# Three-layer kernel on one core: first product cut 384 + 192 tokens, its result stored in units of 192 tokens, some weight loads and front-end steps moved

## The chip, the cores and the metric

One Trainium2 chip, one of its cores. The metric is device time in microseconds of one execution; of several executions the median is taken. The program is built with an instruction scheduler, so the order of the instructions on an engine is partly the scheduler's; the places where the kernel itself fixes an order are named below.

## The reference, cut to what matters

```python
a = phi - np.max(phi, axis=2, keepdims=True)        # phi: 8 batches, 8 heads, 576 tokens, 32 slots
a = np.exp(a)
a = a / (np.sum(a, axis=2, keepdims=True) + 1e-09)
k_m = np.einsum('bhsm,bhsd->bhmd', a, k)            # d = 64
v_m = np.einsum('bhsm,bhsd->bhmd', a, v)
scores = (1.0 / np.sqrt(64)) * np.matmul(q, k_m.transpose(0, 1, 3, 2))
scores = scores - np.max(scores, axis=-1, keepdims=True)
attn = np.exp(scores)
attn = attn / (np.sum(attn, axis=-1, keepdims=True) + 1e-09)
x = np.matmul(attn, v_m)                            # 4608 tokens x 512
...
h = x @ w_in                                        # first layer: 512 -> 2048
r = np.maximum(h, 0.0)
x = (r * r) @ w_out                                 # 2048 -> 512
...
h = x @ w_in2                                       # second layer, the same sizes
return ((h * (1.0 / (1.0 + np.exp(-h)))) @ w_out2).astype(np.float32)
```

## The kernel before, in words

The kernel has four stages: the **first product** (`x @ w_in` with its relu, together with the attention that feeds it), then the **second product** (`g @ w_out`, with g the squared relu), then the two products of the second layer. The last three use seven block products in the place of eight (their blocks are called B11, B21, B12, B22 and the combinations T1 to T4); each matmul in them has 384 columns. A full-precision product is made of three matmuls of type fp32r, on a high and a low part of each factor (hi x hi, hi x lo, lo x hi).

**First product.** Batch by batch (8 batches of 576 tokens), 16 units a batch; a unit is 128 of the 2048 columns of w_in. `first_product(t)` makes unit t: two halves of 288 tokens (`HALF`), each of 6 matmuls 128x288, so 12 matmuls a unit, into a two-bank PSUM tile `h` (two such tiles). ScalarE then applies the relu (L671) into `gt`, which holds two units (f and f + 1), and after every second unit SyncE stores `gt` to the scratch tensor g1 (`to_rows`, L623). The rows of g1 are tiles of 384 tokens, so a batch of 576 falls into a store of 384 and one of 192 tokens. Batch 0 is made otherwise (`first_by_halves`, L637): tokens 0 to 255 and 256 to 575 apart (`SPANS0`), 96 matmuls of 256 columns and 96 of 320.

**Front.** While batch b - 1 is multiplied, `front(b)` prepares batch b: loads of phi, kv and q, `kv_product` (`pskv`, L407), `kv_turn`, then for three ranges r of 192 tokens `scores(r)` (`pssc`; max, exp on ScalarE L483, sum, reciprocal, a scaling on GpSimd) and `transpose_attn(r)` (`et`, then hi by ScalarE L499 and lo by VectorE L500 into `at`, the operand of batch b's units), and four pieces `wp` of w_in multiplied by v_m (`piece`, `pswp`; hi by ScalarE L554, lo by VectorE L555). The tables `PLAN`, `PLAN1` and `PLAN2` say ahead of which unit each step is written. For batch 0, `START` and a list `tail` give the order, with small bf16 matmuls (`hot`) between as fillers. `follow(a, b)` puts a behind b in the order of their engine without a wait; `after` and `hold` add a wait (`hold` for the latest matmul begun).

**Second product.** Its steps are (block product, pair of weight rows) in the order n = 0, 1, 3, 2, 5, 4, 6, four steps for each n. A step is 12 matmuls of 384 columns (L889). Each weight tile `ws` has six slots; slots 2, 5 and 4 hold the weights for T2, B22 and T3. `begin_out1` loads them, and the first quarters `r` of g1, during the last units of the first product; loads of one queue are issued by SyncE in their order.

```python
for r in range(NR):
    at(begin + plan["q"][r], lambda r=r: load_q(r))
    at(begin + plan["scores"][r], lambda r=r: scores(r))
    at(begin + plan["attn"][r], lambda r=r: transpose_attn(r))
```

Of the kernel before, what the change touches and what calls it, by code (L numbers as in the profile page):

```python
# [26 lines left out]
HALF = S // 2  # L27
# [7 lines left out]
TB, TH = 6, 384  # L35
NQ = NF // 2
# [8 lines left out]
CHUNKS0 = ((0, P), (2 * P, 3 * P, S - P))  # L45
SPANS0 = ((0, 2 * P), (2 * P, S))


IDLE = {2: 7, 3: 6, 4: 7}
START = ("phi", "kv", "idle15", "max", "rows", "idle3", "exp", "idle18", "product", "q", "q", "w0", "w1", "q", *(f"w{n}" for n in range(2, 8)))  # L50
UNITS0 = (6, 6, 7, 7, 9, 9, 10, 10)
PIECES0 = {0: (1, 0), 1: (1, 1), 7: (2, 0), 8: (2, 1), 10: (3, 0), 12: (3, 1)}
# [3 lines left out]
    "q": (-5, -3, 5), "scores": (4, 8, 12), "attn": (6, 10, 14), "pieces": (4, 8, 12, 16),  # L56
}
PLAN1 = {
    "phi": -9, "ones": 4, "kv": (-8, -8, -8, -8), "softmax": (1, 2, 3), "product": 5, "turn": 7,
    "q": (-6.5, 4, 9), "scores": (8, 10, 11), "attn": (10, 11, 13), "pieces": (9, 12, 13, 15),  # L60
}
PLAN2 = {**PLAN, "phi": -10, "ones": -5.5, "kv": (-12, -11, -10, -9), "softmax": (-5, -4, -3)}
# [15 lines left out]
def attention_moe_moe(ctx: ExitStack, tc, q, kv, phi, w_in1, w_out1, w_in2, w_out2, out):  # L78
# [199 lines left out]
    def unit(j, i):  # L278
        ins = to_f32(win[:, j, 2 * i:2 * i + 2].rearrange("p k c -> p (k c)"), staged[j, i])
        made[j] = to_f32.last  # L280
        if begun:
            hold(ins)
        else:
            after(ins, ready[(i, 1, 2, 4)[j]])
# [25 lines left out]
    def front(b):  # L310
# [7 lines left out]
        def load_phi():  # L318
            t = st["a"] = lpool.tile([P, NC, 2 * P], F32, tag="a", bufs=2, name="a")
            n = P * (NC - 1) * 2 * P  # L320
            held = hold if b > 1 else in_order
            held(nc.sync.dma_start(t[:, :NC - 1], phi[b, :n].rearrange("(p c e) -> p c e", p=P, e=2 * P)))
            held(nc.sync.dma_start(t[:rows(NC - 1), NC - 1], phi[b, n:].rearrange("(p e) -> p e", e=2 * P)))

        def load_kv(c):


            d = 2 * D + 1
            if c == 0:
                st["kv"] = lpool.tile([P, NC, NP, 2, d], F32, tag="kv", bufs=1, name="kv")  # L330
            n = rows(c)
            t = st["kv"][:n, c]
            (hold if b > 1 else in_order)(nc.sync.dma_start(t.rearrange("p k e d -> p (k e d)"), kv[b, c * P:c * P + n]))
# [11 lines left out]
        def load_q(r):  # L345
            if b == 0:
                if r == 0:
                    st["q"] = apool.tile([P, NP, S], F32, tag="at", name="q")
                in_order(nc.sync.dma_start(st["q"][:, :, r * RT:(r + 1) * RT], q[b, r]))
                return  # L350
            t = st["q", r] = fpool.tile([P, NP, RT], F32, tag="q", bufs=2, name="q")
            (hold if begun else in_order)(nc.sync.dma_start(t, q[b, r]))
# [45 lines left out]
        def kv_product(*gs):  # L398

            ps = bank("pskv")  # L400
            for g in gs:
                st["ps", g] = (ps if g or b else bank("pskv"))[:, g, :2 * D + 1]
            for c, g in ((c, g) for c in range(NC) for g in gs):
                n = rows(c)
                for p in range(NP):
                    h = 2 * p + g
                    mm = pe(nc.tensor.matmul(  # L407
                        st["ps", g][p * M:(p + 1) * M], st["a"][:n, c, h * M:(h + 1) * M], st["kv"][:n, c, p, g],
                        start=(c == 0), stop=(c == NC - 1),
                    ))  # L410
                    join(mm, c == g == p == 0, new=True)
                if b == 0 and g and c in IDLE:
                    idle(IDLE[c])

# [36 lines left out]
        def join(mm, first, new=False):  # L451

            if first and b > 1:
                follow(mm, group["h"] if new else group["last"])
            group["last"] = mm
# [14 lines left out]
        def scores(r):  # L470

            ps = bank("pssc")[:, :, :RT]
            by_heads(ps, 0, lambda p: st["q", r][:, p], st["turned"], new=True)
            nb = 2 * RT // M
            mx = fpool.tile([P, nb, 1], F32, tag="smx", bufs=1, name="smx")
            sm = fpool.tile([P, nb, 1], F32, tag="ssm", name="ssm")
            e = fpool.tile([P, 2, RT], F32, tag="e", bufs=3, name="e")
            for g in range(2):
                nc.vector.transpose(e[:, g], ps[:, g])
            ev = e.rearrange("p g (k m) -> p (g k) m", m=M)  # L480
            nc.vector.reduce_max(mx[:, :, 0], ev, axis=AX.X)
            nc.vector.tensor_tensor(ev, ev, mx.to_broadcast([P, nb, M]), op=ALU.subtract)
            nc.scalar.activation(e, e, AF.Exp, scale=1.0 / float(D) ** 0.5)  # L483
            nc.vector.reduce_sum(sm[:, :, 0], ev, axis=AX.X)
            nc.vector.tensor_scalar_add(sm, sm, 1e-9)
            nc.vector.reciprocal(sm, sm)
            scaled.append(nc.gpsimd.tensor_tensor(ev, ev, sm.to_broadcast([P, nb, M]), op=ALU.mult))
            if r == NR - 1 and "ones" in group:
                follow(scaled[-1], group.pop("ones"))
            st["e", r] = e  # L490

        def transpose_attn(r):
# [6 lines left out]
            nc.scalar.copy(hi, x)  # L499
            nc.vector.tensor_tensor(lo, x, hi.bitcast(F32), op=ALU.subtract)  # L500

        def scores_by_token(r):

            cs = CHUNKS0[r]
            n = len(cs)
            ps = bank("pssc").rearrange("p a n -> p (a n)")[:, :n * 2 * P]
            for i, c in enumerate(cs):
                for p in range(NP):
                    to = i * 2 * P + p * 2 * M
                    pe(nc.tensor.matmul(  # L510
                        ps[:, to:to + 2 * M], st["q"][:, p, c:c + P], st["km"][:, p].rearrange("p g m -> p (g m)"),
# [9 lines left out]
            nc.vector.reduce_max(mx[:, :, :, 0], pv, axis=AX.X)  # L521
# [5 lines left out]
            nc.vector.tensor_tensor(ev, ev, sm.to_broadcast([P, 2 * nb, M]), op=ALU.mult)  # L527
            st["e", r] = e.rearrange("p (g t) -> p g t", g=2)

        def turn_attn(r):  # L530
# [5 lines left out]
            for i, c in enumerate(CHUNKS0[r]):  # L536
                for g in range(2):
                    mm = nc.tensor.transpose(ps[:, g, c - first:c - first + P], st["e", r][:, g, i * P:(i + 1) * P], ident)
                    if r == 0:
                        pe(mm)  # L540
            x = ps[:, :, :end - first]
# [4 lines left out]
        def piece(j, h=None):  # L546
# [10 lines left out]
            by_heads(ps[:, :, :PC], 1, lambda p: win[:, 2 * j + h, p], made[2 * j + h])  # L557
# [4 lines left out]
        if b == 0:  # L562
            third = iter(range(NR))
            do = {
                "phi": load_phi, "kv": lambda: [load_kv(c) for c in range(NC - 1)], "max": max_phi, "rows": max_rows,
                "exp": exp_phi, "product": lambda: kv_product(0, 1), "q": lambda: load_q(next(third)),
# [8 lines left out]
            for w in range(8, 2 * NPC):  # L575
# [3 lines left out]
                lambda: scores_by_token(0), lambda: scores_by_token(1), lambda: (unit(0, 0), unit(0, 1)),  # L579
                lambda: idle(6), lambda: piece(0, 0), lambda: idle(9), lambda: turn_attn(0), lambda: idle(5),  # L580
                lambda: (unit(1, 0), unit(1, 1)), lambda: piece(0, 1),
                lambda: turn_attn(1), lambda: (unit(2, 0), unit(2, 1)), lambda: (unit(3, 0), unit(3, 1)),
            )
            for n, fn in enumerate(tail):
                at(n - 50, fn)
            for n, t in enumerate(UNITS0):
# [29 lines left out]
    def to_rows(b, f, gt):  # L616

        fh, u = divmod(f - 1, NQ)
        i = 0
        while i < S:  # L620
            to, k = divmod(b * S + i, TH)
            n = min(TH - k, S - i)
            nc.sync.dma_start(g1[to // 2][:, 2 * fh + to % 2, u:u + 2, k:k + n], gt[:, :, i:i + n])  # L623
            i += n

    def first_by_halves(t):
# [16 lines left out]
        if half == 0:  # L643
            gts[pair] = gpool.tile([P, 2, S], F32, tag="gt", name="gt")
        nc.scalar.activation(gts[pair][:, :, tk], h[:, :, :n], AF.Relu)
# [3 lines left out]
    def first_product(t):  # L649
# [5 lines left out]
        h = psum.tile([P, 2, 512], F32, tag="h", bufs=2, name="h")  # L655
        j, fo = divmod(f * P, W4)
        for half in range(2):
            tk = slice(half * HALF, (half + 1) * HALF)
            ops = [(g, s, x) for g in range(2) for s, x in ((0, 0), (0, 1), (1, 0))]
            for k, (g, s, x) in enumerate(ops):  # L660
                mm = nc.tensor.matmul(  # L661
                    h[:, half, :HALF], wp[b, j][:, g, s, fo:fo + P], attnT[b][:, x, g, tk],
                    start=(k == 0), stop=(k == len(ops) - 1),
                )
                if half == k == 0:
                    begun.append(mm)
                group["h"] = mm
        if f % 2 == 0:
            gts[b] = gpool.tile([P, 2, S], F32, tag="gt", name="gt")
        gt = gts[b]  # L670
        relus.append(nc.scalar.activation(gt[:, f % 2].rearrange("p (h t) -> p h t", h=2), h[:, :, :HALF], AF.Relu))  # L671
# [121 lines left out]
    def second(src, order, square, to, weights, begin, tiles=tuple(range(10))):  # L793
# [76 lines left out]
        begin(quarters)  # L870
# [4 lines left out]
        for k, (b, n, h) in enumerate(steps):  # L875
            ahead(k + AHEAD)
            bank = BANKS[n]
# [7 lines left out]
            x = cc.pop((b, n, h))  # L885
            for u in range(QS):
# [29 lines left out]
    def begin_out1(quarters):  # L916
# [4 lines left out]
        def held(ins):  # L921
            nonlocal n
            hold(ins, step=min(last, last - EARLY + n * 3 // 4))
            n += 1

        for q in range(WR, WR + 2):
            for k in range(SLOTS):
# [8 lines left out]
        for k in (2, 5, 4):  # L936
            for q in range(WR + 2, NQ):
                held(load_w(w1o, q, k))
# [156 lines left out]
```

## Time and profile before

| | |
|---|---|
| median of 3 executions | 1381.91 us (1380.5 to 1383.04) |
| the profiled execution | 1379.26 us, its span 1377.4 us |
| busy share of TensorE (PE), weight loads (PEld) | 99%, 95% |
| busy share of VectorE (DVE), ScalarE (ACT) | 71%, 58% |
| granted TensorE clock | 1.00 in all stages |

The profile is of one execution; 1.9 us of its time lie outside the span. PE rows are matmuls, PEld rows the loads of their stationary operand, which overlap the matmuls. A matmul's own duration (299 ns for one of 288 columns) is longer than the distance to the next one, since matmuls are pipelined: rates are read from the length of a run of many matmuls. A matmul of type f32 stands in the trace as two instructions, one of type fp32r as one.

### The profile page before, as it was taken

The page shows a single profiled execution, that of the slowest core. Times are in us where ns is not written, and L with a number is a line of the kernel's source. Part 1 is how long each engine was busy: PE and PEld are TensorE (multiplying, and loading weights), DVE is VectorE, ACT ScalarE, POOL GpSimd, SP SyncE. Part 2 cuts the span into 40 slices and gives each one's busy share as a digit, 9 for nine tenths or more (in the row PEclk, how much of TensorE's full clock was granted, in tenths as well). Part 3 has the DMA queues.
Part 4 walks back from the last instruction along what each step waited for, and adds up shares of the span by engine and source line. Part 5 has one row for each costly group of instructions (what it writes and reads, how often), then busy time and mean ns, then how long its engine had stood idle before and what let it go on. Part 6 is the DMA issues. An engine that isn't in the chain of part 4 may idle for free.

```text
span 1377.4 us, 25465 instructions
## 1 busy us (share of the span) xinstructions
PE 1356.8 (99%) x9349; PEld 1311.7 (95%) x9349; DVE 982.6 (71%) x1602; ACT 796.1 (58%) x1305; POOL 21.5 (2%) x44
## 2 busy tenths in 40 slices
PE   8899999999999999999999999999999999999998
PEld 6778888898999999999999999999999999999998
DVE  4768787747797988989565756566449868768583
ACT  3656666667778686777354645555444444444442
POOL 0000000000000000000000000000000000000000
PEclk9999999999999999999999999999999999999999
DMA  9979999899877978899998787888999567574651
GB/s 325 373 248 339 360 362 328 294 346 356 307 256 274 310 256 299 262 310 340 301 322 299 250 308 269 281 287 285 366 399 355 165 217 244 171 238 159 223 157 35
DMA packets 208446, 388.26 MB, mean 282 GB/s; under 512 B 19264, under 2 KB 90944, under 8 KB 208320
## 3 DMA queue, kind: packets, MB, share of 16 engines
q1 hardware_dynamic: 208320, 386.62, 81.2%
q8 instruction: 74, 1.21, 0.4%
q14 instruction: 52, 0.43, 0.1%
HBM read 253.38 MB, written 133.17 MB: 281 GB/s over the span
## 4 chain that ended last, share of the span: by engine, by line
PE 88%; DMA 9%; SPq 1%; ACT 1%; DVE 1%; issue 0%; ACTq 0%; DVEq 0%
PE psa L889 22%; PE psb L889 15%; PE psa L1003 15%; PE psc L889 15%; PE h L661 9%; PE psc L1003 7%; PE psb L1003 4%; DMA st<-moe_w_in 2%; DMA a<-phi 2%; DMA g<-gt 1%; DMA w1o<-pp 1%; PE pswp L463 1%; PE pskv L407 1%; DMA q<-q 1%; DMA r<-g 1%; DMA kv<-kv 1%
## 5 line engine op out<-in xcount | busy, mean ns | idle before, releaser
L856 DVE TENSOR_TENSOR c<-r,c 128x768 fp32r<-128x768 f32 x336 | 316.5, 955 | 141.4 <-ACT c L855 140.5
L855 ACT CAST c<-r 128x768 fp32r<-128x768 f32 x336 | 279.7, 837 | 233.9 <-PE psa L889 86.1
L889 PE MATMUL psa<-c,ws 128*128 128x384 f32 x1728 | 310.7, 336 | 1.8 <-ACT c L855 1.5
L889 PEld LDWEIGHTS psa<-c,ws 128*128 128x128 f32 x1728 | 301.8, 188 | 2.4 <-ACT c L855 1.7
L1003 PE MATMUL psa<-xc,ws 128*128 128x384 f32 x1152 | 217.9, 336 | 0.0
L889 PE MATMUL psc<-c,ws 128*128 128x384 f32 x1152 | 207.9, 335 | 0.0
L661 PEld LDWEIGHTS h<-at,wp 128*128 128x128 f32 x1344 | 180.1, 188 | 28.7 <-ACT gt L671 16.7
L889 PE MATMUL psb<-c,ws 128*128 128x384 f32 x1152 | 206.3, 336 | 0.0
L1003 PEld LDWEIGHTS psa<-xc,ws 128*128 128x128 f32 x1152 | 202.3, 188 | 0.0
L889 PEld LDWEIGHTS psc<-c,ws 128*128 128x128 f32 x1152 | 201.3, 188 | 0.0
L889 PEld LDWEIGHTS psb<-c,ws 128*128 128x128 f32 x1152 | 201.2, 188 | 0.0
L661 PE MATMUL h<-at,wp 128*128 128x288 f32 x1344 | 190.9, 299 | 4.4 <-ACT gt L671 4.2
L1003 PE MATMUL psc<-xc,ws 128*128 128x384 f32 x576 | 110.8, 335 | 0.0
L1003 PEld LDWEIGHTS psc<-xc,ws 128*128 128x128 f32 x576 | 101.1, 188 | 0.0
L671 ACT ACTIVATE gt<-h 128x576 f32<-128x576 f32 x112 | 72.2, 648 | 35.7 <-PE h L661 25.9
L205 DVE TENSOR_TENSOR pp<-pw,pp 128x256 f32<-128x256 f32 x148 | 63.1, 436 | 32.7 <-ACT pp L204 30.4
L833 ACT ACTIVATE r<-r 128x768 f32<-128x768 f32 x96 | 80.7, 843 | 4.2 <-PE psc L889 3.4
L162 ACT CAST top<-st 128x256 f16<-128x256 bf16 (+1 forms) x112 | 57.9, 526 | 30.5 <-PE psa L1003 12.9
L204 ACT CAST pp<-pw 128x256 fp32r<-128x256 f32 x148 | 58.0, 402 | 29.5 <-PE psa L1003 15.4
L1017 ACT ACTIVATE g2t<-g2t 128x1152 f32<-128x1152 f32 x48 | 54.7, 1164 | 28.1 <-DVE g2t L733 28.1
L166 DVE SCALAR_TENSOR_TENSOR pw<-st,top 128x256 int32<-128x256 int32 x96 | 41.2, 435 | 28.6 <-ACT top L162 28.0
L1003 PE MATMUL psb<-xc,ws 128*128 128x384 f32 x288 | 56.9, 336 | 0.0
(103 smaller groups left out, 1164.3 us busy)
## 6 DMA issues: line engine op xcount, KB each, us to landing
r<-g SPq DMA_DIRECT2D x192, 384.0 KB, 5.8
g<-g2t SPq DMA_DIRECT2D x48, 768.0 KB, 7.0
ws<-w2i SPq DMA_DIRECT2D x136, 256.0 KB, 5.1
ws<-w2o SPq DMA_DIRECT2D x136, 256.0 KB, 4.4
ws<-w1o SPq DMA_DIRECT2D x116, 256.0 KB, 4.5
g<-gt SPq DMA_DIRECT2D x64, 384.0 KB, 5.9
kv<-kv SPq DMA_DIRECT2D x32, 516.0 KB, 6.2
st<-moe_w_out SPq DMA_DIRECT2D x64, 256.0 KB, 5.5
```

The lines of the kernel that those rows point to most:

```text
L162: ins = nc.scalar.copy(top.bitcast(F16).rearrange("p (n h) -> p n h", h=2)[:, :, 1], flat.bitcast(BF16).rearrange("p (n h) -> p n h", h=4) ...
L166: to_f32.last = nc.vector.scalar_tensor_tensor(f.bitcast(I32), flat.rearrange("p (n w) -> p n w", w=2)[:, :n, 1], 13, top, op0=ALU.logical ...
L204: held(nc.scalar.copy(hi, w[:, of]))
L205: tt(lo, w[:, of], hi.bitcast(F32), op=ALU.subtract)
L661: mm = nc.tensor.matmul(h[:, half, :HALF], wp[b, j][:, g, s, fo:fo + P], attnT[b][:, x, g, tk], start=(k == 0), stop=(k == len(ops) - 1),)
L671: relus.append(nc.scalar.activation(gt[:, f % 2].rearrange("p (h t) -> p h t", h=2), h[:, :, :HALF], AF.Relu))
L833: ins = nc.scalar.activation(x, x, AF.Square)
L855: nc.scalar.copy(c[:, 0], r(name))
L856: tt(c[:, 1], r(name), c[:, 0].bitcast(F32), op=ALU.subtract)
L889: mm = nc.tensor.matmul(ps[o][bank], W[h * QS + u][:, slot(n), wi, o * P:(o + 1) * P], x[:, xi, u], start=(first and h == u == m == 0), st ...
L1003: mm = nc.tensor.matmul(ps[q][bank], W[q][:, slot(n), wi, k * P:(k + 1) * P], x[:, xi, k], start=(n in FIRST and k == 0 and m == 0), stop= ...
L1017: nc.scalar.activation(gq[q][:, :3], gq[q][:, :3], AF.Silu)
```

## The change

- **g by units of 192 tokens.** `gt` is laid out as 3 ranges of 192 tokens, in each range both units of a pair next to each other; a store then writes runs of 2 x 192 (or 4 x 192) values where it wrote runs of 192 or 384. The second product reads its operand as two runs of 192 columns. The PSUM tile `h` is now one stretch of 576 columns that crosses the border of two banks (`HB`), and so a unit is 6 matmuls of 384 columns and 6 of 192, where it was 12 of 288.
- **Batch 0.** `SPANS0` becomes tokens 0 to 191 and 192 to 575, so 96 matmuls of 192 columns and 96 of 384. Its q is loaded in two contiguous pieces; the first units begin ahead of the second piece of w_in, and the second range's max comes behind the first range's scaling.
- **Softmax and transposes.** The exp of `scores(r)` is a step of its own (`softmax(r)`), written one unit later from batch 2 on and put behind the latest relu on ScalarE, as is the cast in `transpose_attn`; the transposes come one unit later (7, 11, 15 for 6, 10, 14). `PLAN1` and `PLAN2` change, `join` gets new cases.
- **Queues.** q is laid out contiguously for each range; loads of kv for batch 2 and phi for batch 3 are put behind the last q of batch 1.
- **Second product.** Slots 2, 5 and 4 of weight rows 4 to 7 are loaded after steps 1, 3, 5, 7, 9 and 11 of the second product; the others start up to 6 matmul groups later.

```diff
-HALF = S // 2
+HB = 512 - TH
...
-CHUNKS0 = ((0, P), (2 * P, 3 * P, S - P))
-SPANS0 = ((0, 2 * P), (2 * P, S))
+CHUNKS0 = ((0, RT - P), (RT, RT + P, S - P))
+SPANS0 = ((0, RT), (RT, S))
...
-    "q": (-5, -3, 5), "scores": (4, 8, 12), "attn": (6, 10, 14), "pieces": (4, 8, 12, 16),
+    "q": (-5, -3, 5), "scores": (4, 8, 12), "attn": (7, 11, 15), "pieces": (4, 8, 12, 16),
...
+            if b == 2:
+                follow(ins, group["q"])
...
-            nc.scalar.activation(e, e, AF.Exp, scale=1.0 / float(D) ** 0.5)
+            st["e", r] = e, ev, sm, nb
+
+        def softmax(r):
+
+            e, ev, sm, nb = st["e", r]
+            ins = nc.scalar.activation(e, e, AF.Exp, scale=1.0 / float(D) ** 0.5)
+            if b > 1:
+                follow(ins, relus[-1])
...
-            nc.scalar.copy(hi, x)
+            ins = nc.scalar.copy(hi, x)
+            if b > 1:
+                follow(ins, relus[-1])
...
+            at(begin + plan["scores"][r] + (1 if b > 1 else 0), lambda r=r: softmax(r))
...
-            to, k = divmod(b * S + i, TH)
-            n = min(TH - k, S - i)
-            nc.sync.dma_start(g1[to // 2][:, 2 * fh + to % 2, u:u + 2, k:k + n], gt[:, :, i:i + n])
-            i += n
+            to, half = divmod(b * NR + j, 2)
+            n = min(2 - half, NR - j)
+            rows = g1[to // 2][:, 2 * fh + to % 2, u:u + 2].rearrange("p u n -> p (u n)")
+            nc.sync.dma_start(
+                rows[:, half * 2 * RT:(half + n) * 2 * RT], gt[:, j:j + n].rearrange("p j u n -> p (j u n)"),
+            )
+            j += n
...
-        h = psum.tile([P, 2, 512], F32, tag="h", bufs=2, name="h")
+        h = psum.tile([P, 2, 512], F32, tag="h", bufs=2, name="h").rearrange("p a n -> p (a n)")[:, HB:HB + S]
         j, fo = divmod(f * P, W4)
-        for half in range(2):
-            tk = slice(half * HALF, (half + 1) * HALF)
+        for tk in (slice(0, TH), slice(TH, S)):
...
-        relus.append(nc.scalar.activation(gt[:, f % 2].rearrange("p (h t) -> p h t", h=2), h[:, :, :HALF], AF.Relu))
+        relus.append(nc.scalar.activation(gt[:, :, f % 2], h.rearrange("p (j n) -> p j n", n=RT), AF.Relu))
...
-                            ps[o][bank], W[h * QS + u][:, slot(n), wi, o * P:(o + 1) * P], x[:, xi, u],
+                            ps[o][bank].rearrange("p (j n) -> p j n", n=RT) if square else ps[o][bank],
+                            W[h * QS + u][:, slot(n), wi, o * P:(o + 1) * P], x[:, xi, u],
...
-        for k in (2, 5, 4):
-            for q in range(WR + 2, NQ):
-                held(load_w(w1o, q, k))
+        return {
+            4 * i + 2 * j + 1: [lambda k=k, q=q: hold(load_w(w1o, q, k)) for q in (WR + 2 * j, WR + 2 * j + 1)]
+            for i, k in enumerate((2, 5, 4)) for j in range(2)
+        }
```

Three places show what moves. The first is TensorE in the middle of batch 0, where batch 1's kv product (`pskv`), its turn (`pst`), pieces of w_in (`pswp`) and batch 0's units (`h`) alternate. Before:

```order
L637 MATMUL h<-at,wp 128x320 x12
L407 MATMUL pskv<-kv,a 32x129 x40
L463 MATMUL pswp<-win,kvm 32x256 x8
L637 MATMUL h<-at,wp 128x256 x2
L637 MATMUL h<-at,wp 128x320 x2
L435 MATMUL pst<-ident,y_604 128x128 x2
```

And now:

```order
L677 MATMUL h<-at,wp 128x192 x12
L481 MATMUL pswp<-win,kvm 32x256 x8
L677 MATMUL h<-at,wp 128x384 x12
L423 MATMUL pskv<-kv,a 32x129 x40
L677 MATMUL h<-at,wp 128x192 x12
L677 MATMUL h<-at,wp 128x384 x12
L451 MATMUL pst<-ident,y_643 128x128 x2
```

The piece stands 12 matmuls ahead of the kv product, and 24 whole matmuls of units stand between the kv product and its turn, where there were 4.

The second place is SyncE's queue late in batch 0: the stores of g, the last q of batch 1 and the five loads of kv for batch 2. Before:

```order
L333 DMA kv<-kv 128x1032 x4
L333 DMA kv<-kv 64x1032
L623 DMA g_0_100<-gt 128x2x384
L352 DMA q<-q 128x768
L623 DMA g_0_100<-gt 128x2x192
```

And now:

```order
L661 DMA g_0_100<-gt 128x768
L661 DMA g_0_100<-gt 128x384
L365 DMA q<-q 128x768
L338 DMA kv<-kv 128x1032 x4
L338 DMA kv<-kv 64x1032
```

The q load has moved ahead of the five kv loads.

The third place is ScalarE at the last range of attention, that of batch 7 (`e` the exp, `at` the cast of the transposed attention, `gt` the relu of one unit). Before:

```order
L554 CAST wp<-pswp 128x2x512
L483 ACTIVATE e<-e 128x384
L162 CAST top<-st 128x256
L671 ACTIVATE gt<-h 128x576
L162 CAST top<-st 128x256
L671 ACTIVATE gt<-h 128x576
L204 CAST pp<-pw 128x256
L499 CAST at<-et 128x2x192
L671 ACTIVATE gt<-h 128x576 x2
```

And now:

```order
L713 ACTIVATE gt<-h 128x3x192
L506 ACTIVATE e<-e 128x384
L162 CAST top<-st 128x256
L713 ACTIVATE gt<-h 128x3x192
L204 CAST pp<-pw 128x256
L713 ACTIVATE gt<-h 128x3x192
L524 CAST at<-et 128x2x192
L713 ACTIVATE gt<-h 128x3x192
L587 CAST wp<-pswp 128x2x512
```

Counted from the end of the first product, 18 relus stood behind this `at` cast before and 17 stand behind it now; batch 7 itself has 16.

## Rows read from the trace of the kernel before

**Rows 1.** Windows: length, busy us (instructions) of PE, PEld, DVE, ACT, POOL, clock, DMA.

```profile
20.00:35.80 15.80, 12.24 (x127) 9.09 (x126) 12.49 (x23) 9.13 (x15) 0.00 (x0) 1.00 1.04 373
35.80:74.60 38.80, 35.36 (x434) 27.96 (x434) 29.53 (x65) 25.04 (x42) 2.58 (x5) 1.00 0.97 355
74.60:158.00 83.40, 79.98 (x926) 67.74 (x919) 58.04 (x135) 52.59 (x103) 5.66 (x9) 1.00 0.90 317
158.00:290.00 132.00, 132.00 (x1460) 114.99 (x1459) 105.24 (x240) 90.44 (x175) 10.36 (x15) 1.00 0.95 331
290.00:320.00 30.00, 27.18 (x199) 26.15 (x198) 4.72 (x10) 20.69 (x33) 0.00 (x0) 1.00 1.02 365
```

**Rows 2.** Waits of PE, 35.8 to 320 us: us in total, times, longest.

```profile
PE h L661 <- ACT gt L671: 4.2, 6, 1.1
PE pssc L463 <- DMA q<-q: 1.5, 1, 1.5
PE psa L889 <- ACT c L855: 1.5, 1, 1.5
PE h L637 <- ACT wp L559: 1.2, 1, 1.2
PE pswp L463 <- DVE e L479: 0.5, 1, 0.5
PE psa L889 <- DVE c L856: 0.4, 1, 0.4
```

**Rows 3.** The chain, one row; then PE's timeline in four short windows: start, length, run.

```profile
453.69 8.36 PE psc L889 x48
...
36.64 2.65 PE L637 MATMUL h<-at,wp 128*128 128x320 f32 x17
215.82 4.41 PE L661 MATMUL h<-at,wp 128*128 128x288 f32 x32
30.95 2.31 PE L637 MATMUL h<-at,wp 128*128 128x256 f32 x18
18.16 2.29 PE L510 MATMUL pssc<-km,q 128*128 128x64 f32 x19
```

**Rows 4.** Groups by shape, PE and PEld, first 325 us: busy, mean ns, idle before.

```profile
L661 PEld LDWEIGHTS h<-at,wp 128*128 128x128 f32 x1344 | 180.1, 188 | 28.7 <-ACT gt L671 16.7 <-ACT at L499 5.0 <-issue 3.7
L463 PEld LDWEIGHTS pswp<-win,kvm 64*32 64x32 f32 x576 | 9.6, 106 | 4.3 <-issue 2.0 <-PE pswp L463 0.9 <-DVE wp L555 0.3
L510 PEld LDWEIGHTS pssc<-km,q 128*128 128x128 f32 x40 | 4.6, 192 | 0.3 <-DMA q<-q 0.3
L463 PE MATMUL pswp<-win,kvm 64*32 64x512 f32 x448 | 30.8, 593 | 0.5 <-DVE e L479 0.5
L463 PE MATMUL pswp<-win,kvm 64*32 64x256 f32 x128 | 5.4, 385 | 1.1 <-DVE ssm L525 1.1
```

**Rows 5.** Timeline of SP, ACT and PE around two waits.

```profile
53.03 3.46 SPq L333 DMA_DIRECT2D kv<-kv  x5
57.41 0.33 SPq L352 DMA_DIRECT2D q<-q  x1
...
103.40 0.51 ACT L499 CAST at<-et 128x384 fp32r<-128x384 f32 x1 [0.88 <-DVE et L498]
104.73 1.20 ACT L671 ACTIVATE gt<-h 128x576 f32<-128x576 f32 x2
...
105.43 1.85 PE L661 MATMUL h<-at,wp 128*128 128x288 f32 x12 [1.08 <-ACT gt L671]
```

**Rows 6.** Timeline at the turn to batch 7, and to the second product.

```profile
288.75 0.56 DVE L500 TENSOR_TENSOR at<-et,at 128x384 fp32r<-128x384 f32 x1 [0.27 <-ACT at L499]
292.30 0.67 ACT L671 ACTIVATE gt<-h 128x576 f32<-128x576 f32 x1
...
314.10 3.45 PE L661 MATMUL h<-at,wp 128*128 128x288 f32 x24 [0.86 <-ACT gt L671]
319.00 0.62 PE L889 MATMUL psa<-c,ws 128*128 128x384 f32 x2 [1.46 <-ACT c L855]
```

More of the change, by code (lines that the diff above doesn't have):

```diff
@@ L280, in unit @@
         made[j] = to_f32.last
-        if begun:
+        if j > 3:
             hold(ins)
         else:
-            after(ins, ready[(i, 1, 2, 4)[j]])
+            after(ins, ready[(0, 1, 2, 4)[j]])
+            if j == 1:
+                follow(to_f32.last, ready[3])
     k0 = fpool.tile([P, NP, 2, M], F32, tag="et", bufs=1, name="km")
@@ L410, in kv_product @@
                     ))
-                    join(mm, c == g == p == 0, new=True)
+                    join(mm, c == g == p == 0, new=True, second=True)
                 if b == 0 and g and c in IDLE:
@@ L449, in kv_turn, with join @@
                 ready.append(ins)
-        def join(mm, first, new=False):
-            if first and b > 1:
+        def join(mm, first, new=False, second=False):
+            if first and (b > 1 or new and b == 0 and begun):
                 follow(mm, group["h"] if new else group["last"])
+            elif first and b == 1 and second:
+                follow(mm, group["last"])
             group["last"] = mm
@@ L505, in scores_by_token @@
             n = len(cs)
+            first, end = SPANS0[r]
+            qr = st["q"][:, NP * first:NP * end].rearrange("p (k n) -> p k n", k=NP)
             ps = bank("pssc").rearrange("p a n -> p (a n)")[:, :n * 2 * P]
@@ L562, in front @@
         if b == 0:
-            third = iter(range(NR))
+            part = iter(range(2))
             do = {
                 "phi": load_phi, "kv": lambda: [load_kv(c) for c in range(NC - 1)], "max": max_phi, "rows": max_rows,
-                "exp": exp_phi, "product": lambda: kv_product(0, 1), "q": lambda: load_q(next(third)),
+                "exp": exp_phi, "product": lambda: kv_product(0, 1), "q": lambda: load_q(next(part)),
             }
@@ L578, in front @@
                 lambda: (kv_scale(0), kv_scale(1)), kv_turn, lambda: idle(7),
[L579 to L582, printed above, removed]
+                lambda: scores_by_token(0), lambda: (unit(0, 0), unit(0, 1)), lambda: idle(6), lambda: piece(0, 0),
+                lambda: scores_by_token(1), lambda: idle(3), lambda: turn_attn(0), lambda: idle(5),
             )
@@ L585, in front @@
                 at(n - 50, fn)
+            for n, fn in enumerate((
+                lambda: (unit(1, 0), unit(1, 1)), lambda: piece(0, 1), lambda: (unit(2, 0), unit(2, 1)),
+            )):
+                at(0.1 + n / 10, fn)
+            at(1.1, lambda: (turn_attn(1), unit(3, 0), unit(3, 1)))
             for n, t in enumerate(UNITS0):
@@ L643, in first_by_halves @@
         if half == 0:
-            gts[pair] = gpool.tile([P, 2, S], F32, tag="gt", name="gt")
-        nc.scalar.activation(gts[pair][:, :, tk], h[:, :, :n], AF.Relu)
+            gts[pair] = gpool.tile([P, NR, 2, RT], F32, tag="gt", name="gt")
+        first, end = (i // RT for i in SPANS0[half])
+        nc.scalar.activation(
+            gts[pair][:, first:end].rearrange("p j u n -> p u j n"), h[:, :, :n].rearrange("p u (j n) -> p u j n", n=RT), AF.Relu,
+        )
         if half:
@@ L869, in second @@
         start = len(begun)
-        begin(quarters)
+        later = begin(quarters) or {}
         for k in range(SQUARES):
@@ L876, in second @@
             ahead(k + AHEAD)
+            for fn in later.get(k, ()):
+                fn()
             bank = BANKS[n]
@@ L922, in held @@
             nonlocal n
-            hold(ins, step=min(last, last - EARLY + n * 3 // 4))
+            hold(ins, step=min(last, last - EARLY + 6 + n * 3 // 4))
             n += 1
         for q in range(WR, WR + 2):
-            for k in range(SLOTS):
+            for k in (0, 1, 3):
                 held(load_w(w1o, q, k))
```

62 lines of the change are left out of this document (41 added, 21 removed).

## The prediction, made before the changed kernel ran

> **What bounds the kernel now.** I first read the windows [rows 1]. From 158 to 290 us TensorE is busy for 132.00 of 132.00 us: work added to its stream there makes the kernel longer by as much. From 35.8 to 158 us it is idle for 3.4 and 3.4 us, and about the turn to the second product for 2.8 us; between 20 and 35.8 us VectorE is busy for 12.5 of 15.8 us and TensorE runs fillers between. So what can be taken away in the first 320 us is small. The list of waits [rows 2] says what it is: from 35.8 us on, 4.2 us in six waits for a relu, 1.5 us in one wait for a load of q, 1.2 us for the cast of a piece of w_in, and 1.5 + 0.4 + 0.5 us that hang on casts and on VectorE. Everything behind 320 us keeps its matmuls. The question is thus whether TensorE's stream grows by more than these waits.
>
> **TensorE's stream.** The rates come from runs of matmuls [rows 3]. 48 of 384 columns take 8.36 us, 174.2 ns each. For the others I take off the last one's own 0.30 us: 320 columns 2.35/16 = 147 ns, 288 columns 4.11/31 = 132.6 ns, 256 columns 2.01/17 = 118 ns. These four lie near a line of 0.44 ns a column. 192 columns don't occur in this type and with a full 128x128 weight. Along the line they would take 118.2 - 64 x 0.45 = 89 ns: the lower end. But the run of 64 columns, also with a full weight of its own for each, takes 1.99/18 = 111 ns, far above the line. What holds it is seen in the weight loads [rows 4]: one of 32 columns lasts 106 ns, one of 128 columns 188 ns in the fp32r matmuls and 192 ns in the run of 64. That is 82 ns for 96 columns, so some 109 ns of 128 columns' loading that the next load has to wait for. At 256 columns and more this is covered by the matmul; at 192 (89 ns) it isn't. I take 111 ns, the row in which the weight load rules; the upper end is 118 ns, that of 256 columns.
>
> The Trainium skill, TensorE: Matmul & The Clock Gate, section LDWEIGHTS, states P / 1.2 ns for P columns; an estimate of 107 ns for 128, which would make the sum below 3 us smaller. It speaks against cutting 576 columns as 384 + 192.
>
> A pair of matmuls of 288 columns takes 265.2 ns, a pair of 384 and 192 takes 174.2 + 111 = 285.2 ns: 20.0 ns more. Seven batches with 16 units of 6 pairs are 672 pairs: **+13.4 us**. Batch 0: 96 matmuls grow from 320 to 384 columns, 96 x 27.3 ns = +2.6 us; of the 96 that shrink from 256 to 192, the first 24 are made while VectorE's chain sets the pace, the other 72 give 72 x 7.2 ns = -0.5 us: **+2.1 us**. Together +15.5 us; at 89 ns it would be -1.3 + 0.5 = -0.8 us, at 118 ns +18.1 + 2.6 = +20.7 us. Each ns on the matmul of 192 columns is worth 0.74 us.
>
> **What is taken away.** (1) The last q of batch 1 was issued at 57.41 us behind five kv loads issued from 53.03 us [rows 5], and TensorE waited 1.5 us for it. It now goes ahead of them: -1.5 us. The kv loads that are now late by one issue (0.33 us [rows 5]) are for batch 2; no wait for kv is among the waits [rows 2], so an issue more is taken as covered, and would cost its 0.33 us if it weren't. (2) The wait of 1.2 us for the cast of a piece stands between kv product and turn, where only 4 matmuls of units covered it; 24 stand there now: -1.2 us. (3) Of the relu waits, the one of 1.08 us at 105.43 us shows the cause: the relu runs only from 104.73 us, behind an `at` cast that had itself waited 0.88 us for VectorE [rows 5]. With cast and exp behind the relu that is gone, but the 1 us casts of pieces may still stand ahead of a relu; I take three quarters of 4.2 us: -3.2 us, with ends of 2 and 4.2. (4) The waits for `c` (1.5 + 0.4 us) stay: the first cast `c` still comes behind the last relu [rows 6]. (5) The start: fewer scores stand ahead of the first units, but VectorE has the same work up to the second range's `at` (12.5 us busy of 15.8 [rows 1], and the rest mostly waits of the softmax chain for ScalarE and TensorE), and the second range is what all later units need. I take -0.4 us; the ends are 0 and -3.3, the idle time that VectorE has there. Sum: **-6.3 us**, between -4.7 and -10.2.
>
> **What costs nothing.** The g stores and the q loads are as many bytes in longer runs; transfers are hidden but for (1). The 12 weight loads that move into the second product are issued after steps 1 to 11; a step is 12 x 174.2 ns = 2.09 us, and the first weight moved is used at step 14, 13 steps or 27 us later, so they land under matmuls; if they didn't, each step would wait for its own. Behind them on SyncE's queue wait loads of r for batch 1 of the second product, wanted 58 us later. The operand read in two runs: matmuls that read 512 columns as two runs of 256 last 593 ns, those of one run of 256 last 385 ns [rows 4], 0.81 ns a column, with no step at the border; I take nothing for it, and 3 ns on each of 2016 matmuls, 6 us, as the upper bound. The relu writes three runs in place of one: ScalarE is busy for 90 of 132 us [rows 1], so nothing.
>
> **A new wait.** At the turn to batch 7 the last `at` is complete at 288.75 + 0.56 = 289.3 us, while the batch's first relu starts at 292.30 us [rows 6] and its unit, 12 matmuls or 1.6 us and some 0.2 us of way earlier, at about 290.5: a slack of 1.2 us. The cast now stands one relu later, a unit of 6 x 285.2 = 1.7 us. So the second matmul of the batch, which reads the low part, waits some 0.3 to 0.5 us, and behind it the whole stream. For six batches (2 to 7), **+2.1 us**; the ends are 0 and 6 x 1.2 = 7 us, if VectorE has other work just then.
>
> **Sum.** 15.5 - 6.3 + 2.1 = +11.3 us on the profiled execution's 1379.26 us gives 1390.6; the median shown is 2.65 us above that execution, so **1393 us**. Its own range is 1386 (108 ns, most waits gone) to 1401 (118 ns).
>
> **The rivals.** *The weight load doesn't bind* (faster): if loads of fp32r weights overlap each other enough, 192 columns cost 89 ns, the stream is 0.8 us shorter, and -0.8 - 6.3 + 2.1 = -5.0 us gives 1377. It decides below 96 ns for the matmul of 192 columns. For it: the runs of fp32r matmuls follow the line down to 256 columns, and the 111 ns come from another type, f32. Against it: weight loads of both types last the same (188 and 192 ns). The Trainium skill, same page, section Back-to-back issue gap, gives sustained distances of 81 ns for 128 columns and 131 ns for 512, by which 192 columns would be some 89 ns, an estimate; but it would have 384 columns near 115 ns, where the trace has 174. *The turn of the batch binds*: the low part of `at` comes a unit too late in every batch; 6 x 1.2 us in place of 2.1 gives +5.1, 1398 us. For it: the slack of 1.2 us is less than a unit; against it: units get longer, which gives ScalarE and VectorE time. *The waits are not what the change removes* (it doesn't do what it says): the relu waits stay behind the pieces' casts, and only q and the piece are gained: -3.1 in place of -6.3, 1396 us. *A middle*: 192 columns between 92 and 99 ns, or nearly all waits and the start's 3.3 us gained with 105 ns: within 0.2%.
>
> **Chances.** About 0.2%, 2.8 us, is what a measurement of this kernel tells from no change. Forecast 0.52, turn 0.11, waits kept 0.10: all slower, 0.73. Weight load doesn't bind 0.18, faster. Middle 0.09. For 8 in 10 the range must reach to the first rival: 1377 to 1401 us.
>
> **What would show it.** The distance of the 192 column matmuls in an unbroken run (111 ns: right; 90 ns: the sum's first term is wrong); the matmuls of a batch's 16 units, now 16 x 12 x 132.6 ns = 25.5 us, would take 1.9 us more; no wait for q and none for a relu above 0.5 us from 60 to 160 us; waits of TensorE for `at` at the batch turns, of which the trace before has none; the second product still 174.2 ns a matmul, which a slower two-run operand would raise for 350 us.

## The result, and the profile after

Six executions of the changed kernel took 1387.82 to 1391.74 us, median **1389.57 us**; six of the kernel before 1380.07 to 1383.28 us, median 1382.47 us. The ratio is 1.0051 [1.0040, 1.0063]: **7.1 us slower**, where 11.3 us were forecast, and inside the range. The profiled execution took 1390.73 us, its span is 1388.9 us.

TensorE's runs first. In the timeline the columns are start, length, operation and count. The first two fences are of the changed kernel, the six matmuls of 192 columns of one unit and a long run of whole units; the third is the same long run with the cut at 288 (experiment 2).

```profile
297.04 0.81 PE L703 MATMUL h<-at,wp 128*128 128x192 f32 x6
```

```profile
295.89 31.61 PE L703 MATMUL h<-at,wp 128*128 128x384 f32 x216
```

```profile
289.23 29.01 PE L704 MATMUL h<-at,wp 128*128 128x288 f32 x216
```

Less the last one's own 0.27 us, five distances between matmuls of 192 columns take 0.54 us, 108 ns each. Over all units the first of the five is 88 ns in the median and the others are 111 to 113 ns; in return the second matmul of 384 columns starts 200 ns after the first, where the next ones follow after 174 or 175. So the mean of a whole unit is what counts. The two long rows hold 108 pairs and differ by 2.60 us: 24 ns a pair here, where 20.0 were forecast (the last four units of the batch last 1.79 to 1.88 us). From start to start, units without other work between them most often last 1.72 us for 1.59 before, some 21 ns a pair.

The windows of the changed kernel, with the columns of [rows 1]; the first two stretches begin and end with TensorE's first unit of batch 1, of batch 4, and the first matmul of the second product:

```profile
76.27:192.22 115.95, 115.12 (x1283) 100.67 (x1282) 84.88 (x194) 72.75 (x140) 8.40 (x12) 1.00 0.92 328
192.22:328.96 136.74, 135.28 (x1293) 123.02 (x1289) 83.18 (x185) 89.67 (x169) 8.04 (x11) 1.00 0.86 301
```

And of the kernel before, cut at the same events:

```profile
74.60:188.73 114.13, 110.71 (x1291) 94.21 (x1283) 85.75 (x196) 73.08 (x142) 8.29 (x13) 1.00 0.94 331
188.73:319.00 130.27, 127.82 (x1292) 114.37 (x1288) 81.24 (x185) 89.64 (x169) 7.72 (x11) 1.00 0.95 330
```

Batches 4 to 7 are longer by 6.47 us. Batches 1 to 3, with three quarters as many matmuls of the kind, by only 1.82 us: their TensorE is busy for 4.4 us more, and 2.6 us of idle time are gone. Where they went is in the list of waits of TensorE from 35.8 to 330 us (us in total, times, longest), which answers to [rows 2]:

```profile
PE psa L935 <- ACT c L897: 1.5, 1, 1.5
PE pswp L481 <- DVE mx L392: 0.9, 1, 0.9
PE h L703 <- ACT gt L713: 0.8, 2, 0.5
PE pst L451 <- ACT y L439: 0.6, 1, 0.6
PE pssc L481 <- PE pswp L481: 0.4, 1, 0.4
PE psa L935 <- DVE c L898: 0.4, 1, 0.4
```

The waits for q and for the piece's cast are gone, the relu waits are 0.8 us where they were 4.2, and none for `at` has come. But three new ones (0.6, 0.4 and 0.9 us, at 56.2, 57.7 and 73.1 us) stand in the preparation of batch 1, where those for q and the piece stood.

The second product keeps its rate with the operand in two runs: a row of the chain (start, length, matmuls), and the largest group of its matmuls in 320 us of it, in the changed kernel (335 to 655 us) and in the one before (325 to 645 us), where the operand is one run (count, busy us, mean ns).

```profile
373.22 8.36 PE psa L935 x48
```

```profile
L935 PE MATMUL psa<-c,ws 128*128 128x384 f32 x781 | 140.0, 336 | 0.0
```

```profile
L889 PE MATMUL psa<-c,ws 128*128 128x384 f32 x781 | 140.0, 336 | 0.0
```

One thing was not in the forecast at all: two stretches of the profiled execution at half clock (granted clock 0.51 and 0.50, so 1.2 of 2.4 GHz), each 3.4 us long. Windows, of the start and of the start of the second product:

```profile
33.00:36.40 3.40, 3.40 (x26) 1.85 (x25) 1.51 (x3) 2.32 (x4) 0.00 (x0) 0.51 1.02 233
...
330.00:333.40 3.40, 3.40 (x11) 3.40 (x12) 3.40 (x5) 2.57 (x4) 0.00 (x0) 0.50 0.97 347
```

**The two profiled executions set side by side:** first unit of batch 1 at 76.27 us for 74.60 (+1.7), from there to the second product 252.7 us for 244.4 (+8.3: TensorE's busy time +11.9, its idle time -3.6), from there to the end 1059.9 us for 1058.4 (+1.5, the second half-clock stretch). That is +11.5 us, more than the medians' +7.1, because the execution profiled before (1379.26 us) was 3.2 us below the median of its six, and the one after 1.2 us above. So single terms of this comparison are good to some 2 us; the experiments go by medians.

### The profile page after: what moved, and what is told of

Same layout as the page of the kernel before. It is cut to its first block, busy times and chain, and to the rows that moved or that the text cites. A ratio compares the mean times of both kernels' runs of the same rounds, so it can differ in the third digit from the quotient of the medians.

```text
span 1388.9 us, 25455 instructions
## 1 busy us (share of the span) xinstructions
PE 1372.8 (99%) x9341; PEld 1329.5 (96%) x9341; DVE 985.1 (71%) x1602; ACT 795.7 (57%) x1305; POOL 22.2 (2%) x44
## 4 chain that ended last, share of the span: by engine, by line
PE 94%; DVE 2%; DMA 2%; ACT 1%; SPq 0%; issue 0%; POOL 0%; ACTq 0%; POOLq 0%
PE psa L935 22%; PE psb L935 14%; PE psa L1051 14%; PE psc L935 14%; PE h L703 13%; PE psc L1051 7%; PE psb L1051 4%; PE pswp L481 2%; DMA kv<-kv 1%; PE pskv L423 1%; PE h L677 1%; PE pssc L481 1%; ACT top L162 0%; DVE win L166 0%; PE pst L451 0%
## 5 line engine op out<-in xcount | busy, mean ns | idle before, releaser
L703 PEld LDWEIGHTS h<-at,wp 128*128 128x128 f32 x1344 | 196.1, 190 | 22.8 <-ACT gt L713 14.8
L703 PE MATMUL h<-at,wp 128*128 128x384 f32 (+1 forms) x1344 | 203.7, 308 | 0.8 <-ACT gt L713 0.8
```

Source lines behind the costliest of these rows:

```text
L703: mm = nc.tensor.matmul(h[:, tk], wp[b, j][:, g, s, fo:fo + P], attnT[b][:, x, g, tk], start=(k == 0), stop=(k == len(ops) - 1),)
```

## The experiments

Theory **A**, that of the prediction after the result: the split 384 + 192 alone costs the time; the other edits take away waits. Rival **B**: the slowdown comes from the other edits (the store and operand layout, or the moved steps). Rival **C**: the rest saves nothing, and the relu waits went because units got longer. Medians of the kernel before were 1381.8 to 1383.5 us in the four groups of runs.

**1. The split alone, in the kernel before.**

```diff
-        h = psum.tile([P, 2, 512], F32, tag="h", bufs=2, name="h")
+        h = psum.tile([P, 2, 512], F32, tag="h", bufs=2, name="h").rearrange("p a n -> p (a n)")[:, 512 - TH:512 - TH + S]
...
-            tk = slice(half * HALF, (half + 1) * HALF)
+        for tk in (slice(0, TH), slice(TH, S)):
```

> The kernel before with one edit: a unit of batches 1 to 7 is cut 384 + 192 tokens in place of 288 + 288; stores, batch 0 and all orders stay. Theory (the weight load paces matmuls of 192 columns at 111 ns): 672 pairs grow by 18 to 20 ns, +12 to +13 us of TensorE's stream, and up to 3 us of relu waits in batches 1 and 2 are absorbed by the longer units: +9 to +13 us on the kernel before. Rival (the slowdown comes from the start, from the clock, or from the moved steps): within 2 us of the kernel before.

Measured 1389.44 us, ratio 1.0050 [1.0039, 1.0062], 6.7 us: all of the slowdown. It is below the range of A (9 to 13 us), since batches 1 to 3 take up much of it (table below). Its relu waits are 1.0 us, with ScalarE's order as before:

```profile
PE h L660 <- ACT gt L670: 1.0, 3, 0.6
```

**2. The whole change with the cut at 288.**

```diff
+CUT = 288
+HB = 512 - CUT
...
-        for tk in (slice(0, TH), slice(TH, S)):
+        for tk in (slice(0, CUT), slice(CUT, S)):
```

> The changed kernel with one edit: a unit is cut 288 + 288 again, in a PSUM stretch that crosses the bank border after 288 columns; g by units of 192 and everything else stay. Theory: the stream loses 12 us against the changed kernel and keeps the gains of the moved steps; 1377 us, 0.3 to 0.5% faster than the kernel before; waits at the batch turns of up to 2 us may appear, since the units are shorter. Rival (another part costs): 1387 to 1390.

1382.19 us, 0.9997 [0.9986, 1.0008], where A had 1377: B is out, and so is A's gain. The waits are there again; list of waits, then ScalarE's and TensorE's timeline at the largest of them (in brackets: idle before, and what ended it):

```profile
PE h L704 <- ACT gt L714: 4.4, 6, 1.6
...
PE pswp L482 <- DVE mx L393: 0.9, 1, 0.9
PE pst L452 <- ACT y L440: 0.8, 1, 0.8
```

```profile
103.12 0.51 ACT L525 CAST at<-et 128x384 fp32r<-128x384 f32 x1 [0.88 <-DVE et L524]
103.54 1.00 ACT L588 CAST wp<-pswp 128x1024 fp32r<-128x1024 f32 x1
104.44 0.65 ACT L714 ACTIVATE gt<-h 128x576 f32<-128x576 f32 x1
```

```profile
105.15 1.86 PE L704 MATMUL h<-at,wp 128*128 128x288 f32 x12 [1.58 <-ACT gt L714]
```

This is the place of [rows 5], with the moved order: the relu that is late still stands behind an `at` cast that waits 0.88 us for VectorE, and behind the 1.00 us cast of a piece. The cast was put behind the latest relu written; the relu that suffers is the next one.

**3. The whole change with the cut at 320** (the same edit, `CUT = 320`): parts of 320 and 256, unequal but none below 256.

> The changed kernel with units cut 320 + 256 tokens. Theory (only a matmul shorter than its weight load costs): 147 + 118 ns a pair, the same as 288 + 288, so within 1 us of that kernel, 1377 us. Rival (unequal parts or the switch between two lengths cost, each switch some ns): between it and the changed kernel, 1380 to 1390.

1381.37 us, 0.9995 [0.9985, 1.0004]: as with 288, though not the 1377 us expected. It isn't the unequal parts that cost, but the short one.

**4. g by units of 192 alone, in the kernel before.** The store, the layout of `gt` and the two-run operand of the change, units of 288 in the stretch across two banks.

```diff
-            nc.sync.dma_start(g1[to // 2][:, 2 * fh + to % 2, u:u + 2, k:k + n], gt[:, :, i:i + n])
...
+            nc.sync.dma_start(
+                rows[:, half * 2 * RT:(half + n) * 2 * RT], gt[:, j:j + n].rearrange("p j u n -> p (j u n)"),
+            )
...
-        for half in range(2):
-            tk = slice(half * HALF, (half + 1) * HALF)
+        for tk in (slice(0, HALF), slice(HALF, S)):
```

> The kernel before with g stored by units of 192 tokens, both rows of a pair together, and read as two runs of 192 columns; units stay 288 + 288, batch 0 keeps its spans (its relus are cut at the borders of units, 16 more small activations). Theory: stores land under matmuls and the two-run operand costs nothing: within 2 us of the kernel before; the six wait for relus may shrink by the 0.9 us that hung on a store. Rival (longer runs relieve the queues in the first 70 us): 2 to 4 us faster; rival (two-run operand costs): 3 us or more slower.

1381.64 us, 0.9993 [0.9980, 1.0006]: nothing, as the prediction had it.

**5. The softmax and transpose steps alone, in the kernel before.**

```diff
-    "q": (-5, -3, 5), "scores": (4, 8, 12), "attn": (6, 10, 14), "pieces": (4, 8, 12, 16),
+    "q": (-5, -3, 5), "scores": (4, 8, 12), "attn": (7, 11, 15), "pieces": (4, 8, 12, 16),
...
+            ins = nc.scalar.copy(hi, x)
+            if b > 1:
+                follow(ins, relus[-1])
```

> The kernel before with the softmax edit alone: the exp one unit later and behind the latest relu, the cast of the transposed attention behind the latest relu, the transposes one unit later; units stay 288 + 288. Theory after the runs so far (the order takes no relu wait away; in the changed kernel they went because its units are longer): waits of TensorE for a relu stay near 4 us between 75 and 160 us, the time within 2 us of the kernel before, or up to 3 us slower if the waits at the turn to the third batch come here too. Rival, the prediction's own step: the relu waits fall by 3 us and the kernel is 2 to 3 us faster.

1381.96 us, 1.0000 [0.9987, 1.0013]. The waits for the relu are not fewer, and the one of [rows 5] stands where it stood:

```profile
PE h L671 <- ACT gt L681: 6.0, 8, 1.1
```

```profile
105.39 1.85 PE L671 MATMUL h<-at,wp 128*128 128x288 f32 x12 [1.07 <-ACT gt L681]
```

**6. The reverse: experiment 2 with these steps as before.**

> The changed kernel with units of 288 + 288 and the softmax steps as before (exp and cast free, transposes at 6, 10, 14). Theory: batch 3 loses the 2.8 us that it took longer in the kernel with 288 + 288 alone, so 1379 to 1380 us; the relu waits stay near 4 us. Rival: the 2.8 us come from another moved step, and stay: 1382.

1381.72 us, 0.9992 [0.9983, 1.0002]: the same as with them, and not the 1379 to 1380 us expected; the relu waits are 6.5 us. A's explanation of the relu waits has fallen. C stands: over all profiled executions, with either order, the relu waits are 3.2 to 6.5 us in the ten kernels whose units are cut 288 + 288 or 320 + 256, and 0 to 1.0 us in the four with 384 + 192 or 432 + 144.

**7. The cut at 432 (432 + 144), one execution.** If the weight load sets the pace, 144 columns must take as long as 192.

> The changed kernel with units cut 432 + 144 tokens, to measure the matmul of 144 columns. Theory (the weight load paces): 111 ns, the same as for 192 and for 64 columns; 432 columns 195 ns, so a pair takes 306 ns against 265 for two of 288, and the kernel is some 27 us longer than the one with 288 + 288, 15 us longer than the changed one. Rival (192 columns lie on a slope of their own): 144 columns nearer to 70 to 90 ns.

1402.21 us. Five matmuls of 144 columns in the timeline, (0.72 - 0.28)/4 = 110 ns each:

```profile
313.98 0.72 PE L704 MATMUL h<-at,wp 128*128 128x144 f32 x5
```

64 columns (type f32) 111 ns [rows 3], 144 columns 110, 192 columns 111: a flat floor. 432 columns take 197 ns, so a pair is 307 ns and 576 columns cost 42 ns more than as 288 + 288. The kernel is 20 us longer than experiment 2, where some 27 were expected: batches 4 to 7 take 144.07 us, 15.1 more, but batches 1 to 3 take 120.94 us, only 5.5 more.

That the weight load is what sets this floor is argued, not shown: the runs changed the length of the moving operand and never the weights. A rival is a fixed price of each matmul instruction. Against it stands a run of the changed kernel, 80 matmuls of 129 columns, each with a weight load of its own, but of 32 columns:

```profile
49.25 2.55 PE L423 MATMUL pskv<-kv,a 128*32 128x129 f32 x80
```

That is some 29 ns each, so a matmul instruction with a load of its own can be far cheaper than 111 ns.

**8. q ahead of kv, alone, in the kernel before.**

```diff
+            if b == 2:
+                follow(ins, group["q"])
```

> The kernel before with the load of batch 1's last q ahead of batch 2's kv loads (and batch 2's kv and ones at the changed kernel's times). Theory: the wait of 1.5 us for q goes, but it stands in the stretch of batch 0 that also waits for casts and VectorE; a part comes back as other waits: 0 to 1.5 us faster. Rival: the whole 1.5 us are gained, and the first unit of batch 1 starts 1.5 us earlier.

The edit also writes the kv loads of batch 2 two to five units later, as the changed kernel does.

1382.33 us, 1.0003 [0.9990, 1.0017]. The wait for q is gone, its 1.5 us are not gained. In the trace the first unit of batch 1 starts at 72.32 us, 2.3 us earlier than before, but that of batch 4 at 190.65, 1.9 us later. The relu waits are 6.4 us, which alone says little, since they are 6.0 to 6.5 us in experiments 4 to 6 too.

```profile
PE h L667 <- ACT gt L677: 6.4, 8, 2.3
```

So something beside TensorE's stream seems to pace batches 1 to 3 of this kernel. A candidate is the preparation of w_out that runs between the units from unit 20 on (`WOUT0`; casts on ScalarE, subtractions on VectorE), on the two engines that the late relus wait behind. Three runs begin it ten units later.

**9, 10 and 12. `WOUT0 = 30`** in the kernel before (9), in experiment 2 (10) and in the whole change (12).

```diff
-WOUT0 = 20
+WOUT0 = 30
```

> The kernel before with the preparation of w_out (its loads, casts on ScalarE, differences on VectorE, stores) begun ahead of unit 30 in place of unit 20. Theory (in the first three batches ScalarE's queue and the transfers, not TensorE's stream, set the pace, so that every version reaches batch 4 at 189 to 191 us): with less beside them the relu waits between 90 and 160 us shrink, batch 4 starts 1 to 3 us earlier; 1379 to 1381 us, unless the preparation then ends too late for the second product. Rival (these batches are held by the order of the front's own steps): batch 4 starts at 189 us as before, the time stays.

> The changed kernel with units of 288 + 288 and the preparation of w_out begun ahead of unit 30. Theory: as for the run before, batch 4 at 187 to 189 us in place of 190.8; 1379 to 1381 us, which would be faster than the kernel before by 0.1 to 0.25%. Rival: 1382.

> The changed kernel, units 384 + 192, with the preparation of w_out begun ahead of unit 30. Theory (TensorE's stream is 12 us longer, and some 5 us of that were hidden in batches 0 to 3 because the work beside them set the pace there): with that work taken out of the first batches the split's price shows nearly in full: 9 to 12 us over the same kernel with 288 + 288 (1377.8), so 1387 to 1390, within 2 us of the changed kernel although the 288 + 288 kernel gained 4 us from the same edit. Rival (the moved start saves the same in both): 1385, 4 us less than the changed kernel.

(9) 1381.02 us, 0.9981 [0.9972, 0.9991]; (10) **1377.78 us, 0.9959 [0.9947, 0.9972]**, faster than both kernels; (12) 1389.13 us, 1.0048 [1.0031, 1.0065]. Windows from the first unit of batch 1 to that of batch 4 and from there to the second product, of experiment 2, then of 10, then of 12:

```profile
75.27:190.76 115.49, 110.90 (x1284) 94.30 (x1283) 84.22 (x194) 72.74 (x141) 8.29 (x12) 1.00 0.92 324
190.76:319.71 128.95, 127.39 (x1292) 114.31 (x1288) 82.38 (x185) 89.51 (x169) 7.86 (x11) 1.00 0.89 318
```

```profile
75.09:185.60 110.51, 109.36 (x1284) 94.10 (x1283) 80.46 (x178) 69.70 (x130) 8.35 (x12) 1.00 0.91 321
185.60:316.99 131.39, 127.89 (x1292) 114.38 (x1288) 89.67 (x201) 92.19 (x179) 7.82 (x11) 1.00 0.93 327
```

```profile
77.20:191.73 114.53, 114.53 (x1284) 100.50 (x1283) 81.60 (x181) 70.61 (x131) 8.26 (x12) 1.00 0.89 313
191.73:328.08 136.35, 134.90 (x1292) 122.88 (x1288) 88.44 (x198) 92.95 (x178) 8.02 (x11) 1.00 0.88 314
```

The same stretches in the versions that matter here, in us:

| | batches 1 to 3 | batches 4 to 7 |
|---|---|---|
| before | 114.13 | 130.27 |
| the change | 115.95 | 136.74 |
| 1, split alone | 116.19 | 136.94 |
| 2, change with 288 | 115.49 | 128.95 |
| 9, before, w_out later | 110.56 | 133.18 |
| 10, change with 288, w_out later | 110.51 | 131.39 |
| 12, change, w_out later | 114.53 | 136.35 |

With w_out begun early, batches 1 to 3 take 114 to 116 us with 288 + 288 as with 384 + 192. With it later, 288 columns take 110.5 us and the split 4.0 us more: there, the preparation of w_out did pace them. It isn't free later on: with 288 columns batches 4 to 7 take 2.4 to 2.9 us more with it.

From batch 1 to the second product TensorE is busy for 12.1 us more with the split (the change against experiment 2), and for 12.2 us more with w_out later (12 against 10). Of that 3.9 and 3.2 us go into time in which TensorE had been idle, so in these executions the split costs 8.3 and 9.0 us. By medians it costs 0.0054 x 1382 = 7.5 us with w_out early and 0.0089 x 1382 = 12.3 us with it later, each good to some 2 to 3 us by the intervals. So the split's price is 12 us of TensorE's time, some of it hidden where other engines set the pace; that moving w_out uncovers as much as the medians say is not shown by the traces.

**11. Experiment 2 with 15 small bf16 matmuls written between the last unit and the second product**, to fill TensorE's idle 1.5 us ahead of the second half-clock stretch; they are extra work.

```diff
+            if square and k == 0:
+                y = W[0][:, 0, 0].bitcast(BF16)
+                for _ in range(15):
+                    nc.tensor.matmul(ps[0][bank][:, :2 * P], y[:, :P], y[:, :2 * P], start=True, stop=True)
```

> The changed kernel with units of 288 + 288 and 15 small bf16 matmuls on TensorE between the last unit and the second product, where it sits idle for 1.5 us; their results are overwritten. Theory (the half clock of 3.4 us that several profiles show 1 us after this turn comes of that idle time): no stretch at half clock near 321 us, and 0.5 to 1.5 us off the median. Rival: the clock falls there all the same, since the stretch before was idle enough, or the fillers run late and delay the first product: no gain or 1 us slower.

1381.76 us, 0.9986 [0.9976, 0.9996]; experiment 2 had 0.9997 [0.9986, 1.0008], so a gain of 1 us is neither shown nor excluded. Its profile has no half clock there, but one execution says little: that of the kernel before had none either.

## Why the prediction was right in its direction and too high by 3 to 4 us

**The stream: right.** 192 columns were taken at 111 ns and, the first distance of each run apart, take 111 ns; the pair costs some 21 ns more in undisturbed units, for 20.0. TensorE's busy time grew by 11.9 us from batch 1 on, 18 ns a pair, where 13.4 were summed. So the rival *the weight load doesn't bind* fell by its own sign: it needed less than 96 ns. That it is the load which binds remains argued (experiment 7). The Trainium skill, TensorE: Matmul & The Clock Gate, section LDWEIGHTS, gives P / 1.2 ns for P columns, by an estimate 107 ns for 128. Experiment 7 agrees in kind (110 ns at 144 columns, as at 192) and is 3 ns above it. The Trainium skill's figures on the same page, section Back-to-back issue gap, would give some 89 ns at 192 columns and 115 at 384, an estimate. They don't hold for these fp32r matmuls, which take 111 and 174 ns.

**What is taken away, (3): the step that failed.** "With cast and exp behind the relu that is gone": the order takes away no wait (experiments 5 and 6). The waits went because a unit lasts 0.12 us longer: experiment 1, with the old order, has 1.0 us of them. So the -3.2 us stand in the trace (4.2 to 0.8 us), under a wrong cause. I read one wait as the work of the one cast ahead of it; two things stood there, the cast that waited for VectorE and the 1 us cast of a piece.

**(1) and (2), q and the piece.** Both waits are gone, as forecast, and no gain is left of them: 1.9 us came back as other waits in the same stretch, and q alone (experiment 8) gave nothing by the end. An idle time on TensorE was taken as time that ends with its wait; that ScalarE and VectorE were behind by as much is the likely reason, since two of the three waits that came back are for them. All edits but the split are worth 0.0003 x 1382 = 0.4 us, within its interval nothing (experiment 2); -6.3 were summed.

**The new wait at batch turns: wrong.** 2.1 us were forecast, none came. The step named the wrong reader: "the second matmul of the batch, which reads the low part". The last range is tokens 384 to 575, which only the unit's second part reads, and the low part is first read by the eighth matmul. The timeline of experiment 2 shows it, VectorE's and then TensorE's: seven matmuls run ahead of the wait.

```profile
154.12 0.56 DVE L528 TENSOR_TENSOR at<-et,at 128x384 fp32r<-128x384 f32 x1 [0.58 <-ACT at L525]
```

```profile
153.16 1.39 PE L704 MATMUL h<-at,wp 128*128 128x288 f32 x7
154.74 2.27 PE L704 MATMUL h<-at,wp 128*128 128x288 f32 x15 [0.19 <-DVE at L528]
```

**The sum.** By medians the split costs 7.5 us, where 13.4 + 2.1 were summed for the stream, because batches 1 to 3 were not TensorE's alone: part of the longer stream went into time in which TensorE had been idle. The forecast subtracted the waits (-6.3) as a gift of the other edits, when it is the split that used up those for the relu. The stream's term was 8.0 us too high and the new wait 2.1 us; the other way, 5.9 us too much were taken away. Together that is 4.2 us too high. Single terms were off by more than the sum, so that it came this near is in part luck.

Batch 0 was forecast at +2.1 - 0.4 - 1.5 - 1.2 = -1.0 us, since the waits for q and the piece stand in it; the trace has +1.7. It is a weak test: without a half-clock stretch its end lies at 74.96 to 75.27 us in experiments 2, 3, 6, 7 and 10, with one near 32 us at 76.27 to 77.20 (the change, 11, 12), and the batch 0 of the kernel before ends at 74.60 us there and at 73.24 in experiment 1.

**What costs nothing: right.** The layout (experiment 4), the two-run operand (8.36 us for 48 matmuls, 336 ns of their own, both as before) and the moved weight loads: TensorE waits for no load of `ws` in the whole span.

**Open.** Which single step paces batches 1 to 3 beside w_out was not tried, nor a weight load of another size; nor is it known why executions of one kernel at a granted clock of 1.00 still differ by 2 us and more.

## What to carry to other kernels

Before a matmul's moving operand is cut, look for the floor: here matmuls with 128 columns of weights of their own took 110 to 112 ns at 64, 144 and 192 columns alike. Look for the shortest matmul with such weights in the trace, however foreign, and check it with a still shorter one. A wait of the busiest engine is a gain only as far as no other engine is behind by the same time; delay that engine's background work first (here 0.4% together with the other edits), and then see what the wait is worth. Before a wait is priced, find the one instruction that reads the late data, and its place in its group.

## What the runs showed of the hardware that was not expected

**Half-clock stretches come and go from one execution to the next.** Of 14 profiled executions, eight have one of 3.4 us right at the start of the second product, after TensorE's idle time there of 1.5 to 1.7 us: from the first matmul of the second product they need 1059.9 to 1060.2 us. The six without need 1058.4 to 1058.6 us, and five of these had the same idle 1.5 us (the kernel before among them); the sixth is experiment 11. In the first 100 us seven of the 14 have one too, of 3.4 or 6.8 us, the earliest at 23 and the latest at 96 us. So one stretch at the second product's start is worth 1.5 us, the idle time alone doesn't decide it, and a difference of 0.1% between two profiles may be nothing else.

**The rates of fp32r matmuls, each with a weight load of its own:** 110 to 111 ns at 144 and 192 columns, 118 at 256, 132.6 at 288, 147 at 320, 174 at 384, 197 at 432. Behind a change of length one distance is off: the second of 192 columns starts only 88 ns after the first, the second of 384 columns 200 ns after the first.
